# First batch worked by halves of the sequence, with an order written out by hand

## The chip, the core and the metric

The kernel runs on one core of a Trainium2 chip. The core has five engines with a queue each: TensorE (PE in the profile, with its weight loads listed apart as PEld), VectorE (DVE), ScalarE (ACT), GpSimd (POOL) and SyncE (SP), which here only issues transfers. The metric is the time of one execution in microseconds, lower is better; the median over several runs counts.

## What is computed

There are 4 batches, 8 heads, 768 positions and 64 columns per head. Keys are taken in 24 chunks of 32. Every query bounds its product with each chunk from above, keeps the six best causal chunks, and attends to these alone. The result, as rows of 512 columns, goes through a layer norm and a two-layer MLP with a residual.

```python
k_min, k_max = k_chunks.min(axis=3), k_chunks.max(axis=3)
ub = sum_d(max(q * k_min, q * k_max))            # [B,H,S,24], -1e9 where the chunk is not causal
top_chunks = argsort(ub)[..., -6:]
scores = where(selected & causal, q @ k.T / 8, -1e9)
x = (softmax(scores) @ v) as [B, S, 512]
xn = (x - mean(x)) / sqrt(var(x) + 1e-6) * g_ln
out = x + relu(xn @ w_ch1) @ w_ch2               # 512 -> 2048 -> 512
```

## The kernel before

Two heads make a pair, so there are 16 pairs `g`, four per batch. Positions are cut in six tiles of 128; the first three are half `r=0`, the last three half `r=1`.

Attention of one pair, by function:

- `load_qk` (L175) puts four transfers on SP, two for queries and two for keys, 192 KB each; `load_v` (L186) puts two on POOL.
- `turn` (L198) transposes query and key tiles on PE, four tiles and then two; a whole pair has 12 transposes at L202.
- `prep_q`, `prep_q2` (L207, L230) bring the queries to SBUF and split them for the bound: in float32 for batch 0, in two float16 parts later. `prep_k` (L243) reduces each chunk to its least and largest key (DVE, L251 and L252) and copies the keys (ACT, L253 and L254). `prep_b` (L256) builds the chunk matrix `BD`.
- `bounds` (L269) is PE: L280 in float32 for batch 0, L290 later, for position tiles 1 to 5. `select` (L296) finds the seventh largest bound (DVE, L307) and writes a mask `MN` (L308). `mask_t` (L313) transposes the mask and copies it into `QA` and `QB` (L318, L319), where it sits beside the queries so that the score matmul adds it.
- `scores` (L347) is PE at L359 and the exponential on ACT at L365, in six pieces per pair: two for half 0 and four for half 1. `diag` (L370) clears the upper triangle on POOL; `values` (L377) is PE at L385; `normalise` (L390) is DVE at L395 and L396 and writes `x_all`.

Then, per batch: `stats` (L405: L417 to L419), `rstd`, `x_t` (L431), `mlp1` (L446: PE at L454, ACT at L458) and `mlp2` (L462: PE at L467, DVE at L474, then the output on SP).

The order comes from numbers written beside each piece of work. `at(t, fn, ...)` records a piece at time `t`, the pieces are emitted in order of `t`, and a scheduler in the framework may still move instructions on each engine between them. One unit of `t` is about a pair. The pairs of batch 0 stand at `t` = -4 to 0 and their preparation before that; the MLP of batch 0 begins after the last of them, at `e = 4.0 * b`:

```python
e = 4.0 * b + (GAP if b > 0 else 0.0)
...
for m in range(KT2):
    at(e + 0.05 + 0.5 * d * m / KT2, mlp1, b, m // 8, 2 * m % KT2)
for n in range(24):
    at(e + 0.06 + 0.5 * d + 0.5 * d * n / 24, mlp2, b, n // 4, n % 4)
```

So batch `b`'s MLP lies among the attention of batch `b+1`, and the last batch's MLP stands alone. PSUM has eight banks: `ps_t` two for transposes, `ps_s` two for bounds and values, `ps_m` two pairs of banks that scores, `mlp1` and `mlp2` share.

The weights are loaded on POOL during batch 0: `w1_load` and `w2_load` first copy one element of a chunk reduction `kc` into the weight tile, so that the transfer starts no sooner than that reduction.

Of the kernel before, what the change touches and what calls it, by code (L numbers as in the profile page):

```python
# [19 lines left out]
def kernel(  # L20
# [21 lines left out]
    NR = 2  # L42
    TR = NT // NR
    HP = H // 2
# [16 lines left out]
    ldp = ctx.enter_context(tc.tile_pool(name="ldp", bufs=4))  # L61
    vap = ctx.enter_context(tc.tile_pool(name="vap", bufs=5))
# [3 lines left out]
    xp = ctx.enter_context(tc.tile_pool(name="xp", bufs=2))  # L66
    xcp = ctx.enter_context(tc.tile_pool(name="xcp", bufs=1))
    htp = ctx.enter_context(tc.tile_pool(name="htp", bufs=1))
# [3 lines left out]
    ps_t = ctx.enter_context(tc.tile_pool(name="ps_t", bufs=2, space=PSUM))  # L72
    ps_s = ctx.enter_context(tc.tile_pool(name="ps_s", bufs=2, space=PSUM))
# [4 lines left out]
    def at(t, fn, *args):  # L78
        pieces.append((t, len(pieces), fn, args))
# [7 lines left out]
    RT = const.tile([P, S], F16, name="RT", tag="RT")  # L87
    hsel = const.tile([P, 2], F32, name="hsel", tag="hsel")
    mhalf = const.tile([P, NT], F32, name="mhalf", tag="mhalf")
    NK = 5  # L90
# [17 lines left out]
    def consts_first():  # L108
        rr = RT[0:64, :]
# [9 lines left out]
        make_identity(nc, ident_f)  # L119
# [4 lines left out]
        )  # L124
        nc.gpsimd.memset(causf, 0.0)
# [4 lines left out]
        nc.vector.memset(hsel[0:64, 1:2], KS)  # L130
        nc.vector.memset(hsel[64:P, 0:1], KS)
        nc.vector.memset(hsel[0:64, 0:1], 0.0)
        nc.vector.memset(hsel[64:P, 1:2], 0.0)
        for i in range(NM):
            nc.vector.memset(MN[i], 0.0)
        for i in range(2):
            ring_init(i)
        nc.vector.tensor_copy(ident_h, ident_f)
        nc.vector.tensor_copy(ident_b, ident_f)

    def consts_late():
        nc.gpsimd.memset(mhalf, -0.5)
# [16 lines left out]
    def w2_load(j, g):  # L159
        nc.gpsimd.tensor_copy(w2b[0:1, 4 * j, 0:1], st[g]["kc"][0:1, 0, 0:1])  # L160
        nc.gpsimd.dma_start(w2b[:, 4 * j:4 * j + 4, :], w2_r[:, 4 * j:4 * j + 4, :])
# [5 lines left out]
    def xb(b):  # L167
        if b not in x_tiles:
            x_tiles[b] = (
                xp.tile([P, NT, H, D], F16, name="x_all", tag="x_all"),  # L170
                xp.tile([P, KT1, S], F16, name="xT", tag="xT"),
            )
        return x_tiles[b]

    def load_qk(g):  # L175
        b, hp = divmod(g, HP)
        for nm, src in (("qn", q), ("kn", k)):
            st[g][nm] = ldp.tile([P, NT, 2, D], F32, name=nm, tag=nm)
            if g == HP:
                nc.gpsimd.tensor_copy(st[g][nm][0:1, 0, 0, 0:1], st[HP - 1]["m8"][0:1, 0, 0, 0:1])  # L180
            for hh in range(2):
                nc.sync.dma_start(
                    st[g][nm][:, :, hh, :], src[b, 2 * hp + hh].rearrange("(t p) d -> p t d", p=P),
                )

    def load_v(g, t0, t1):  # L186
        b, hp = divmod(g, HP)
        if "va" not in st[g]:
            va = st[g]["va"] = vap.tile([P, 2, NT, 80], F16, name="va", tag="va")
            nc.gpsimd.memset(va[:, :, :, D:D + 1], 1.0)  # L190
        va = st[g]["va"]
        for hh in range(2):
            nc.gpsimd.dma_start(  # L193
                va[:, hh, t0:t1, 0:D],
                v[b, 2 * hp + hh, t0 * P:t1 * P, :].rearrange("(t p) d -> p t d", p=P),
            )

    def turn(g, nm, t0, t1):  # L198
        pst = ps_t.tile([P, 512], F32, name="tr", tag="tr")
        src = st[g][nm]  # L200
        for t in range(t0, t1):
            nc.tensor.transpose(pst[:, (t - t0) * P:(t - t0 + 1) * P], src[:, t, :, :], ident_f)  # L202
        return pst[:, 0:(t1 - t0) * P]
# [3 lines left out]
    def prep_q(g, t0, t1):  # L207
        whole = g < HP
        if t0 == 0:
            if whole:  # L210
                for nm in ("q32", "r32"):
                    st[g][nm] = prp.tile([P, S], F32, name=nm, tag=nm)
            else:
                for nm, tag in (("q", "q32"), ("r", "r32")):
                    t2 = prp.tile([P, 2, S], F16, name=nm + "2", tag=tag)
                    st[g][nm + "h"], st[g][nm + "l"] = t2[:, 0], t2[:, 1]
        pst = turn(g, "qn", t0, t1)
        c = slice(t0 * P, t1 * P)
        if whole:
            nc.scalar.copy(st[g]["q32"][:, c], pst)  # L220
            return
        qh, ql = st[g]["qh"], st[g]["ql"]
        u0 = max(t0, 1) * P
        u = slice(u0, t1 * P)
        nc.scalar.activation(qh[:, c], pst, ACTF.Copy, scale=QS)  # L225
        nc.vector.scalar_tensor_tensor(  # L226
            ql[:, u], pst[:, u0 - t0 * P:], QS, qh[:, u], op0=ALU.mult, op1=ALU.subtract,
        )
# [14 lines left out]
    def prep_k(g, t0, t1):  # L243
# [4 lines left out]
        if t0 == 0:  # L248
            st[g]["kc"] = smp.tile([P, 2, NCH], F32, name="kc", tag="kc")
# [311 lines left out]
```

## Time and profile before

| | |
|---|---|
| runs | 330.53, 334.00, 334.06 us; median 334.0 us |
| profiled execution | 332.52 us, span in the profile 330.8 us |
| PE busy / PEld busy | 301.0 us (91%) / 199.2 us (60%) |
| DVE, ACT, POOL busy | 203.9, 180.1, 74.0 us |
| first `mlp1` matmul (L454) | 60.5 us |
| first `mlp2` matmul (L467) | 98.6 us |
| transfers, q and k loads | 64 on SP, 192 KB each, 3.7 and 3.8 us to landing |
| transfers, w1 and w2 | 8 on POOL, 512 KB each, 7.8 and 8.2 us to landing |

A matmul's record spans its way through the array, and these ways overlap; 301 us busy is therefore not 301 us of work, and the time between starts in an unbroken row is what a matmul really occupies. The profile page also cuts the span into 40 slices of 8.27 us with the busy share of each engine in tenths. The chain of waits follows the end of the program back through what released each step.

### The profile page before, as it was taken

The page shows a single profiled execution, that of the slowest core. Times are in us where ns is not written, and L with a number is a line of the kernel's source. Part 1 is how long each engine was busy: PE and PEld are TensorE (multiplying, and loading weights), DVE is VectorE, ACT ScalarE, POOL GpSimd, SP SyncE. Part 2 cuts the span into 40 slices and gives each one's busy share as a digit, 9 for nine tenths or more (in the row PEclk, how much of TensorE's full clock was granted, in tenths as well). Part 3 has the DMA queues.
Part 4 walks back from the last instruction along what each step waited for, and adds up shares of the span by engine and source line. Part 5 has one row for each costly group of instructions (what it writes and reads, how often), then busy time and mean ns, then how long its engine had stood idle before and what let it go on. Part 6 is the DMA issues. An engine that isn't in the chain of part 4 may idle for free.

```text
span 330.8 us, 6794 instructions
## 1 busy us (share of the span) xinstructions
PE 301.0 (91%) x2708; PEld 199.2 (60%) x2708; DVE 203.9 (62%) x657; ACT 180.1 (54%) x261; POOL 74.0 (22%) x116
## 2 busy tenths in 40 slices
PE   3879887999999998999999999999999999899994
PEld 2668675666675664666766565666656455565441
DVE  7766755998857779896564759886634336700121
ACT  2436759677975475358685625377775332366000
POOL 9714835211131422230313131120101020100000
PEclk9999989999999999999999999999999999999999
DMA  9997999963435636424523050000000101000021
GB/s 163 190 187 139 194 195 214 190 146 68 95 26 127 96 93 104 92 45 95 74 51 24 34 87 34 34 33 2 2 0 2 63 34 63 35 0 2 32 95 63
DMA packets 81967, 26.65 MB, mean 81 GB/s; under 512 B 76304, under 2 KB 78352, under 8 KB 81936
## 3 DMA queue, kind: packets, MB, share of 16 engines
q1 hardware_dynamic: 53632, 18.88, 24.1%
q0 software_dynamic: 27776, 7.34, 22.2%
q8 instruction: 21, 0.34, 0.5%
q10 hardware_dynamic: 528, 0.00, 0.1%
q14 instruction: 10, 0.08, 0.1%
HBM read 27.27 MB, written 6.29 MB: 101 GB/s over the span
## 4 chain that ended last, share of the span: by engine, by line
PE 60%; ACT 19%; DVE 15%; issue 2%; DMA 1%; SPq 0%; POOL 0%; ACTq 0%
PE mm L454 20%; PE mm L467 18%; ACT pt L365 8%; PE mm L359 6%; ACT hT L458 5%; PE sm L385 4%; PE ub L280 4%; PE tr L202 3%; ACT KB L254 3%; ACT KA L253 2%; DVE ot L474 2%; PE ub L290 2%; DVE kc L251 2%; DVE kc L252 2%; PE trh L435 2%
## 5 line engine op out<-in xcount | busy, mean ns | idle before, releaser
L365 ACT ACTIVATE pt<-mm 128x1024 f16<-128x1024 f32 x96 | 86.8, 916 | 52.1 <-PE mm L359 51.5
L454 PE MATMUL mm<-xT,w1b 128*128 128x384 f16 x512 | 93.3, 326 | 4.7 <-ACT hT L458 3.2
L467 PE MATMUL mm<-w2b,hT 128*128 128x512 f16 x384 | 92.7, 379 | 2.5 <-DVE ot L474 1.7
L458 ACT ACTIVATE hT<-mm 128x768 f16<-128x768 f32 x64 | 51.8, 810 | 40.7 <-PE mm L454 40.2
L454 PEld LDWEIGHTS <-w1b 128*128 128x128 f16 x512 | 49.0, 98 | 32.3 <-issue 5.5
L467 PEld LDWEIGHTS <-hT 128*128 128x128 f16 x384 | 36.6, 98 | 37.0 <-issue 3.7
L372 POOL TENSOR_SCALAR_AFFINE_SELECT pt<-pt 128x768 f16<-128x768 f16 x32 | 28.2, 880 | 115.4 <-ACT pt L365 115.4
L474 DVE SCALAR_TENSOR_TENSOR ot<-mm,rstd,x_all 128x512 f32<-128x512 f32 x24 | 17.9, 745 | 44.6 <-PE mm L467 43.1
L359 PE MATMUL mm<-QA,KA 128*128 128x128 f16 (+2 forms) x224 | 35.9, 251 | 5.2 <-ACT pt L365 4.3
L359 PE MATMUL mm<-QB,KB 128*128 128x128 f16 (+2 forms) x224 | 35.4, 252 | 0.0
L385 PE MATMUL sm<-va,pt 128*128 128x65 f16 x672 | 33.0, 195 | 2.3 <-ACT pt L365 1.8
L385 PEld LDWEIGHTS <-pt 128*128 128x128 f16 x672 | 28.4, 99 | 9.4 <-ACT pt L365 3.5
L193 POOL DMA_DIRECT2D va<-in_v_dram x32 | 28.2, 883 | 1.1 <-issue 0.2
L395 DVE RECIPROCAL rden<-sm 128x6 f32<-128x6 f32 x32 | 6.2, 193 | 33.5 <-PE sm L385 33.4
L253 ACT CAST KA<-tr 64x512 f16<-64x512 f32 (+1 forms) x32 | 15.0, 468 | 17.3 <-DVE kc L252 17.2
L359 PEld LDWEIGHTS <-KA 128*128 128x128 f16 x224 | 19.0, 102 | 8.9 <-issue 2.3
L202 PE MATMUL tr<-ident_f,qn 128*128 128x128 f32 x96 | 18.7, 303 | 5.9 <-DMA qn<-in_q_dram 5.1
L359 PEld LDWEIGHTS <-KB 128*128 128x128 f16 x224 | 18.6, 101 | 6.7 <-issue 4.2
L202 PE MATMUL tr<-ident_f,kn 128*128 128x128 f32 x96 | 19.7, 306 | 1.6 <-DMA kn<-in_k_dram 0.7
L251 DVE TENSOR_REDUCE kc<-tr 128x16 f32<-128x512 f32 (+1 forms) x32 | 17.7, 552 | 3.1 <-PE tr L202 2.9
L396 DVE TENSOR_TENSOR x_all<-sm,rden 128x384 f16<-128x384 f32 x32 | 17.7, 555 | 0.8
L226 DVE SCALAR_TENSOR_TENSOR q<-tr,q 128x384 f16<-128x384 f32 (+1 forms) x24 | 11.7, 488 | 9.9 <-ACT q L225 9.6
(79 smaller groups left out, 339.8 us busy)
## 6 DMA issues: line engine op xcount, KB each, us to landing
qn<-in_q_dram SPq DMA_DIRECT2D x32, 192.0 KB, 3.7
kn<-in_k_dram SPq DMA_DIRECT2D x32, 192.0 KB, 3.8
out_dram<-ot SPq DMA_DIRECT2D x24, 256.0 KB, 2.0
va<-in_v_dram POOLq DMA_DIRECT2D x32, 96.0 KB, 5.2
w1b<-in_moe_w_ch_dram POOLq DMA_DIRECT2D x4, 512.0 KB, 7.8
w2b<-in_moe_w_ch_dram POOLq DMA_DIRECT2D x4, 512.0 KB, 8.2
gstr<-in_moe_g_ln_dram ACTq DMA_DIRECT2D x1, 2.0 KB, 3.4
```

What stands on the lines that cost most here:

```text
L193: nc.gpsimd.dma_start(va[:, hh, t0:t1, 0:D], v[b, 2 * hp + hh, t0 * P:t1 * P, :].rearrange("(t p) d -> p t d", p=P),)
L202: nc.tensor.transpose(pst[:, (t - t0) * P:(t - t0 + 1) * P], src[:, t, :, :], ident_f)
L251: nc.vector.tensor_reduce(kc[:, 0, n], view, axis=AX.X, op=ALU.min)
L253: nc.scalar.copy(KA[g % NK][0:64, c], pst[0:64, :])
L359: nc.tensor.matmul(sc[:, hh, o:o + w * P], ks[:, t * P:(t + 1) * P], qs[:, s * P:(s + w) * P], start=True, stop=True,)
L365: nc.scalar.activation(pt[:, n0:n1].rearrange("p n h x -> p h n x"), sc[:, :, 0:o].rearrange("p h (n x) -> p h n x", x=P), ACTF.Exp, scale ...
L372: nc.gpsimd.affine_select(out=dv, in_=dv, compare_op=ALU.is_ge, fill=0.0, base=0, pattern=[[0, 2 * TR], [1, P]], channel_multiplier=-1,)
L385: nc.tensor.matmul(pv[:, hh, s2, :], pt[:, where[t, s], hh, :], va[:, hh, t, 0:D + 1], start=(t == 0), stop=(t == s),)
L454: nc.tensor.matmul(hp_[:, i, 0:TR * P], w1b[:, kt, (m + i) * P:(m + i + 1) * P], xT[:, kt, c], start=(kt == 0), stop=(kt == KT1 - 1),)
L458: nc.scalar.activation(hts[b][:, m:m + 2, c], hp_[:, :, 0:TR * P], ACTF.Relu, scale=HS)
L467: nc.tensor.matmul(yp, hts[b][:, kt, s * P:(s + 1) * P], w2b[:, kt, :], start=(kt == 0), stop=(kt == KT2 - 1),)
L474: nc.vector.scalar_tensor_tensor(ot, yp, rs[b]["rstd"][:, s:s + 1], x_all[:, s].rearrange("p h d -> p (h d)"), op0=ALU.mult, op1=ALU.add,)
```

## The change

Batch 0 is no longer worked pair by pair. Its eight units are the four first halves of the sequence and then the four second halves, `u = 0..7`, `g = u % 4`, half `i = u // 4`. The list `begin` writes their order out by hand as steps `n` = -3 to 7: in step `n`, unit `n+3` is turned and reduced, unit `n+2` gets its bounds, unit `n+1` its selection and mask, unit `n` its scores, and unit `n-1` its values. At step 4 the first halves of all heads are done, and their layer norm, `x_t` and `mlp1` follow while the second halves are worked. For these pieces an added dependency ties every instruction on PE, DVE, ACT and POOL to the one before it, so that the scheduler can't move them against each other.

With it come:

- every load of queries and keys is half as long and there are twice as many; keys go first. The second-half keys of batch 0 are gated by a one-element copy on POOL (`load_qk`), and so are the weights;
- values of batch 0 are loaded in halves too; loads have places in a table `loads` by step;
- layer norm, transpose and MLP go by half for all batches: `x`, `xc`, `xT`, `hT` are tiles of a half. `x` is float32, before it was float16. In batch 0 the norm's statistics are taken per pair (`pair_stats`, three instructions of 128 columns a unit) and joined by `bn_aggr`;
- the ReLU of batch 0's queries goes from DVE to ACT, which reads the transposed queries in PSUM a second time;
- PSUM: one pool `ps_t` of four banks for transposes, bounds, values and `mlp2`; `ps_m` keeps its two pairs for scores and `mlp1`;
- eight matmuls on zeros (`warm`) before the first transposes; the exponential's table is asked for at the start (`tiny`); the identity is made before `RT`; `causf` is made later; four rings `QA`, `QB`, `KA`, `KB`, before five;
- `GAP` is 0.8, before 1.5, and MLP pieces of batch `b` lie between `e = 4b + 0.86` and `z = e + 4`: `mlp1` of half 0 in the first half of that stretch, `mlp1` of half 1 and `mlp2` of half 0 in the second, `mlp2` of half 1 in the two units after `z`. For batch 0, `mlp1` of half 0 comes before `e`.

```diff
-    ps_t = ctx.enter_context(tc.tile_pool(name="ps_t", bufs=2, space=PSUM))
-    ps_s = ctx.enter_context(tc.tile_pool(name="ps_s", bufs=2, space=PSUM))
+    ps_t = ctx.enter_context(tc.tile_pool(name="ps_t", bufs=4, space=PSUM))
     ps_m = ctx.enter_context(tc.tile_pool(name="ps_m", bufs=2, space=PSUM))
...
+    def load_qk(g, i):
+        b, hp = divmod(g, HP)
+        for nm, src in (("kn", k), ("qn", q)):
+            t = st[g][nm, i] = ldp.tile([P, TR, 2, D], F32, name=nm, tag=nm)
+            if g < HP and i == 1 and nm == "kn":
+                nc.gpsimd.tensor_copy(t[0:1, 0, 0, 0:1], st[min(g + 1, HP - 1)]["kc"][0:1, 0, 0:1])
+            for hh in range(2):
+                nc.sync.dma_start(...)
...
+    def q_copy(g, i):
+        pst = st[g]["qn", i]
+        if g < HP:
...
+            nc.scalar.copy(st[g]["q32"], pst)
+            nc.scalar.activation(st[g]["r32"][:, u:], pst[:, u:], ACTF.Relu)
...
+    def warm(n):
+        junk = ps_m.tile([P, 2, 512], F32, name="junk", tag="mm")
+        for i in range(n):
+            nc.tensor.matmul(junk[:, i % 2], MN[0][:, 0, :], ..., start=True, stop=True)
...
+    def pair_stats(g, r):
+        for i in range(TR):
+            nc.vector.bn_stats(h["st"][:, i, hp], xh(b, r)[:, i, 2 * hp:2 * hp + 2]...)
...
+    loads = {
+        -3: [(load_v, 0, 0), (load_v, 1, 0)],
+        -2: [(load_v, 2, 0)],
+        -1: [(load_v, 3, 0), (load_qk, 0, 1)],
+        0: [(w1_load, 0, 2), (w1_load, 1, 2), (load_qk, 1, 1)],
+        1: [(load_qk, 2, 1), (w1_load, 2, 3), (w1_load, 3, 3)],
+        2: [(load_v, 0, 1), (load_qk, 3, 1)],
...
+    for n in range(-3, U):
+        there = [0 <= n + d < U for d in range(4)]
+        g, i = zip(*[((n + d) % HP, (n + d) // HP) for d in range(4)])
+        if n > 0:
+            begin += last(n - 1)          # values, normalise, pair_stats
+        if there[0]:
+            begin += [(scores, g[0], i[0], 0), (scores, g[0], i[0], 1)]
+        if n == HP:
+            begin += [(stats, 0, 0, t) for t in range(TR)] + [(centre, 0, 0, t) for t in range(TR)]
+            begin += [(x_t, 0, 0, kt) for kt in range(KT1)]
+        if there[0] and i[0] == 0:
+            begin += [(diag, g[0], 0)]
+        if there[1]:
+            begin += [(select, g[1], i[1])]
+        if there[3]:
+            begin += [(turn, g[3], "kn", i[3]), (k_bound, g[3], i[3]), (k_diag, g[3], i[3])]
+            begin += [(turn, g[3], "qn", i[3]), (q_copy, g[3], i[3]), (k_copy, g[3], i[3])]
...
+        if there[1]:
+            begin += [(mask_t, g[1], i[1]), (mask_ring, g[1], i[1])]
+        if there[3]:
+            begin += [(q_ring, g[3], i[3])]
+        if there[2]:
+            a, z, _ = chosen(g[2], i[2])
+            begin += [(bounds, g[2], s, i[2]) for s in range(a, z)]
...
+        begin += loads[n]
...
+    for n, (fn, *args) in enumerate(begin):
+        pieces.append((-4 + 4.0 * n / len(begin), len(pieces), fn, args, True))
...
+        if b == 0:
+            spread(mlp1, b, 0, ready[0], e)
+            spread(mlp1, b, 1, e + 0.3, m)
+            spread(mlp2, b, 0, e, m)
+            spread(mlp2, b, 1, m, z)
+            continue
+        spread(mlp1, b, 0, e, m)
+        spread(mlp1, b, 1, m, z)
+        spread(mlp2, b, 0, m + 0.01, z)
+        spread(mlp2, b, 1, z + 0.01, z + 2.0)
...
+        for one in done[n:]:
+            if one.engine in (nc.tensor.engine, nc.vector.engine, nc.scalar.engine, nc.gpsimd.engine):
+                if one.engine in ahead:
+                    tc.add_manual_dep(one, ahead[one.engine], order, reason="order")
+                ahead[one.engine] = one.name
```

## The prediction

> **What bounds the kernel now.** I read the slices first, then each stage, then the chain of waits for what a matmul costs. The page's slices of 8.27 us; rows PE, DVE and granted clock:
>
> ```profile
> PE   3879887999999998999999999999999999899994
> DVE  7766755998857779896564759886634336700121
> PEclk9999989999999999999999999999999999999999
> ```
>
> PE is full from the eighth slice on and patchy before. The busy time by stage, cut where the first MLP matmul of batches 0, 1, 2, 3 starts (PE, PEld, DVE, ACT, POOL; clock; transfers), and below it three shorter stretches:
>
> ```profile
> 0.00:60.50 60.50, 45.18 (x444) 37.22 (x445) 40.41 (x143) 33.44 (x50) 32.81 (x66) 0.97 1.31 184
> 60.50:140.30 79.80, 76.45 (x757) 51.28 (x755) 65.08 (x210) 52.21 (x80) 17.85 (x24) 1.00 0.55 101
> 140.30:212.50 72.20, 69.75 (x673) 46.28 (x673) 50.61 (x165) 43.47 (x64) 13.79 (x18) 1.00 0.31 55
> 212.50:282.30 69.80, 67.05 (x608) 42.04 (x606) 38.24 (x122) 38.04 (x52) 8.25 (x9) 1.00 0.06 24
> 60.00:70.00 10.00, 9.75 (x79) 6.39 (x76) 9.72 (x29) 7.48 (x14) 1.84 (x4) 1.00 1.13 186
> 70.00:80.00 10.00, 9.55 (x96) 6.76 (x94) 8.41 (x31) 7.64 (x13) 1.40 (x2) 1.00 0.47 107
> 80.00:90.00 10.00, 9.45 (x91) 6.68 (x88) 8.15 (x29) 8.42 (x14) 1.66 (x2) 1.00 0.35 79
> ```
>
> Pieces of the chain of waits (start, length, what), unbroken rows of matmuls:
>
> ```profile
> 34.66 2.43 PE ub L280 x20
> 61.21 1.09 PE tr L202 x8
> 92.66 0.85 PE sm L385 x28
> 95.34 0.85 PE ub L290 x20
> 287.36 17.55 PE mm L454 x108
> 304.91 17.28 PE mm L467 x80
> ```
>
> Divided: mlp1 0.1625 us a matmul, mlp2 0.216, values 0.030, transposes 0.136, bounds 0.0425 (float16) and 0.122 (float32). By columns a 128-wide score or float16 transpose is 0.055. A pair's PE work is then 12 x 0.136 + 0.85 + 5 x 0.055 + 42 x 0.055 + 42 x 0.030 = 6.3 us (8.0 in batch 0, whose bounds take 2.5); x_t adds 1.35 a batch; MLP 512 x 0.1625 + 384 x 0.216 = 166.1. In all 166 + 33.5 + 3 x 26.7 = 280 us of the 330.8. The other 51 us: 33 us of work in the first 60.5 leaves 27.5 idle; the three mixed stages hold 205 us of work in 221.8, 17 idle (the second of them 68.2 in 72.2, 94.5%); the rest lies in the last stage, of which the last 4.1 us are the last output. So PE bounds the kernel after 60.5 us, and before it a chain does. Its waits in 0 to 60.5:
>
> ```profile
> ACT q L220 <- PE tr L202: 10.6, 3, 4.9
> DVE m L307 <- PE ub L280: 8.8, 4, 3.4
> ACT pt L365 <- PE mm L359: 8.1, 7, 3.6
> ACT KA L253 <- DVE kc L252: 5.4, 5, 2.0
> ```
>
> No engine leads: each stands waiting for another in turn, with DVE busy 40.41 of 60.5, 67%.
>
> **The change, part by part.** PE's work stays: the same transposes, scores and MLP, bounds in equal numbers (4 plus 6 pairs of instructions for 10), some extra causal matmuls (8 for 4, 0.1 each). What moves is where it lies.
>
> *The front goes by DVE.* One step of a first-half unit, from rows of before: L395 0.19, L396 0.555, three statistics of 128 columns; four maxima at 0.1 (ten take 1.0) and mask 0.25 (L308: 0.39 for 240); two reductions of 384 columns (0.55 each, between 0.42 for 256 and 0.69 for 512), 0.2 and 0.26 for the chunk matrix; two mask copies of 256 (0.28, L318: 0.495 for 640); two ring copies of 384 (0.35, L234/L235: 0.54 to 0.60 for 768). The statistics have no row of that size: at least 0.16 (the shortest like it, L418), at most 0.68 (L417, 512 columns); as reductions scale with columns I take 0.28. Sum 5.06; 5.45 with second-half selection. The centring now reads float32: 0.345 (float16 row L419) to 0.48 (L233, 640 float32 columns); I take 0.39.
> DVE starts its first reduction at 8.2 us: ident casts, RT at about 4.1, four rings at 0.84 + 0.22; before, it was 8.0. Steps -3, -2: 2.26 each; -1, 0: 3.47; 1, 2: 5.06; 3: 5.45; into step 4 up to the centred half 4.2: 31.3 us until the first mlp1 matmul. The rest of step 4 to 7, the end of batch 0 and what of pairs 4 and 5 stands among it in DVE's order: 26.3 more, 57.6 in all up to xT of the second half. PE needs 3.1 us of a first-half step (6 transposes, 8 float32 bounds, 10 scores, 12 values) and 5.1 of a second-half one, ACT 3.4 to 3.6 (exponentials 1.62, copies 1.42, ReLU about 0.45, which leaves DVE), and 5.7 in step 4. So DVE sets the pace. A pace without waits doesn't exist; the best comparison is 60 to 90 us of before, DVE 26.3 of 30, 87.6%, in the same company of transposes, selections and matmuls. Then first mlp1 at 8.2 + 31.3/0.876 = 44 us (60.5 before), and end of batch 0's attention E = 8.2 + 57.6/0.876 = 74.
>
> By then PE has done 33.5 + 10.4 (mlp1 of half 0, 64 matmuls) + 3.3 (six half-turns and one bounds of batch 1) = 47 us; idle in the front 27 instead of 27.5, but with 13.7 us more work behind it at 74 than at 60.5. That alone is nothing gained; what counts is what comes after.
>
> *The middle.* Left after E, before the last attention is done: 280 - 47 - 52 = 181 us on PE. DVE's share of it is light: its total 204 + 4, less 65 done and 11 in the tail (15 outputs at 0.745), is 132; ACT's is less. Ratio DVE/PE is 0.73, as in the second mixed stage (50.6/68.2); I take that stage's 94.5%: 191.5 us. The first mixed stage, where DVE had to catch up (65.08), goes away. mlp2 leaves the pairs of banks that scores use; scores then never find one of the two taken. Waits of scores and mlp1 for a free pair cost PE 0.7 + 2.3 us in the mixed stages, so this is worth 3 us at most and I count none of it: mlp2's bank is now taken from the four of transposes, bounds and values.
>
> *The tail.* After the last values PE still has mlp2 of batch 2's second half and all of batch 3: 3 x 16 x 0.216 + 41.5 = 52 us, without DVE or ACT in the way; 1.5 for the stop at the last half's layer norm (before: 0.96 and 0.84 us), then 4.1 to the end. Before it was 42 us of work in 44.4.
>
> *Queues.* SP issues 128 loads for 64, at 0.5 us (0.81 to 1.84: two in 1.03) 32 us more, under 280 us in which SP mostly waits; the price shows where the data is late, see the first rival. In POOL's queue eight diagonals, eight weight loads, the gates and the value loads of batch 0 are in one row. Eight matmuls on zeros lie in the wait for the first load (PE's first 5 us are empty), 0.
>
> Sum: 74 + 191.5 + 52 + 1.5 + 4.1 = 323.1 us span against 330.8. The profiled run took 332.5, 1.7 more than its span, and its median neighbour 334.0. Forecast 324.8 us.
>
> *A rule against it.* PE has 3.1 us of work in a first-half step of 5.8. Before, it fell to half clock in such a stretch (columns as above, granted clock third from the end):
>
> ```profile
> 44.00:46.00 2.00, 1.09 (x10) 1.03 (x10) 1.35 (x5) 1.34 (x2) 1.07 (x3) 1.00 1.24 205
> 48.00:50.00 2.00, 2.00 (x24) 1.81 (x22) 1.51 (x13) 1.02 (x1) 1.11 (x3) 0.50 1.24 206
> ```
>
> At half clock a first-half step is 6.2 us on PE, 0.4 over 5.06/0.876 = 5.8; four such steps cost 1.6 us, which I leave to the range. The Trainium skill (TensorE: Matmul & The Clock Gate, Part 1) lets the clock fall only after an idle window of about 3.4 us. By that rule the sum has no such term; here the longest gap ahead of the fall was 1.24 us, so the row speaks for the range.
>
> **Rivals.**
>
> 1. *Slower: the keys come late.* Second-half keys of pairs 1 to 3 wait for a gate in POOL's queue, behind the step's diagonal, behind ACT's exponentials, and behind weight loads. From a step's start: exponentials done at 3.0, diagonal 0.88, two weight loads with gates 1.5, gate 0.17, SP 0.5, landing 3.8 (median row of kn) to 7.8 (w1b, in the same crowd): 9.9 to 13.9. They are turned 1.1 us into the step after next, 12.7 at my pace. At the slowest landing of w2b, 10.9, they are 4.3 us late in each of steps 2, 3 and 4: E = 87, time 338. It decides from 7.7 us of lateness in all, where E passes 81.7 and the time 332.5. For it: transfers move 184 GB/s over all of 0 to 60.5, more than in any later stage. Against: the halves are 96 KB where 192 took 3.8.
> 2. *No change: three full engines.* From 44 to 74 us the orders hold PE 28, DVE 26 and ACT 28 us of 30, none of which can wait for another. With E = 77 and the third mixed stage's 92% (64.3 in 69.8) for the middle, 196.7: 333 us.
> 3. *Much faster.* DVE at the 97% of 60 to 70 us gives E = 67.6; banks of their own give the middle 98%, 184.7: 311.6 us. Against: nothing in before kept both for long.
>
> That the order isn't what the change says is no rival: the emitted order has all eight mlp1 pieces of half 0 ahead of the second half's x_t.
>
> **How the numbers follow.** Forecast (318 to 330.6) 0.47, much faster 0.20, no change 0.15, slower 0.18. One per cent is about what a measurement of this kernel tells from no change (its runs spread from 330.53 to 334.06); so faster 0.67, same 0.15, slower 0.18. The range leaves a tenth out on each side: 312 to 340, with statistics at 0.68 (24 x 0.4 = 9.6 us on DVE) inside.
>
> **What would show it.** First L490 (mlp1) at 44 us; last xT of batch 0 at 74; last attention value 57.6 us before the span's end; DVE above 80% from 10 to 70 us; no clock of 0.5 after 15 us. Wrong: PE waiting for a kn transfer in steps 2 to 4, or the middle over 197 us with waits of PE for a bank.

## The result, and the profile after

The changed kernel takes 345.32 us (median of 4 runs, 343.13 to 345.52), the kernel before 332.65 us in runs on the same chip. The ratio is 1.037, with a 95% interval from 1.030 to 1.044: slower, where faster was forecast. In this and all later ratios and intervals, runs more than 1.5% above the fastest of the same kernel are left out; the medians are over all runs. The profiled execution took 343.13 us, with a span of 341.4 us against 330.8 before.

The slices of the changed kernel, 8.54 us each, rows PE, DVE and granted clock:

```profile
PE   6693869869599999988779999999999999999995
DVE  7972586566884758899987657996664167010011
PEclk9655589999999999999999999999999999999999
```

Slice four (25.6 to 34.1 us) is the first thing to see: PE falls to 3, and the clock row stands at 5 around it. DVE, which was to be above 80% from 10 to 70 us, never holds that. The stages, cut at the prediction's own milestones (first `mlp1`; last xT of batch 0's second half; last values; end), and two stretches of the front. Columns as before: PE, PEld, DVE, ACT, POOL; then granted clock, share of the transfer engines, GB/s:

```profile
0.00:50.60 50.60, 33.51 (x236) 28.16 (x237) 35.12 (x131) 22.16 (x42) 24.60 (x53) 0.68 0.96 158
50.60:87.70 37.10, 31.20 (x343) 22.65 (x342) 23.91 (x93) 25.59 (x38) 18.64 (x30) 0.98 1.07 123
87.70:284.30 196.60, 183.61 (x1863) 123.70 (x1863) 142.28 (x449) 123.66 (x176) 36.42 (x47) 1.00 0.29 58
284.30:341.40 57.10, 52.89 (x287) 26.92 (x282) 12.23 (x25) 12.98 (x16) 0.85 (x1) 1.00 0.13 47
20.00:30.00 10.00, 7.82 (x64) 7.05 (x63) 7.17 (x31) 5.00 (x9) 3.73 (x10) 0.50 1.01 187
30.00:40.00 10.00, 4.60 (x26) 4.40 (x27) 2.65 (x8) 1.70 (x4) 1.94 (x4) 0.50 0.85 155
```

From 30 to 40 us no engine is busy for half of the time (PE 4.60 of 10 us, DVE 2.65, ACT 1.70), while transfers go on at 155 GB/s. That is the look of a wait for data. The waits of the first 50.6 us name it (engine, line, waited for; us in all, times, longest):

```profile
ACT q L222 <- PE tr L211: 9.5, 4, 6.4
DVE kc L259 <- PE tr L211: 6.9, 2, 6.1
PE tr L211 <- DMA kn<-in_k_dram: 6.7, 2, 6.0
```

Read from the bottom: PE's longest wait, 6.0 us, is for a key transfer (`kn` is a loaded key tile); DVE and ACT wait 6.1 and 6.4 us for the transposes behind it. The same moment in PE's timeline, and then SP's (start, length; idle time before in brackets):

```profile
34.60 0.87 PE L211 MATMUL tr<-ident_f,kn 128*128 128x128 f32 x3 [5.97 <-DMA kn<-in_k_dram]
```

```profile
13.58 0.47 SPq L191 DMA_DIRECT2D kn<-in_k_dram  x1
14.15 10.54 SPq L191 DMA_DIRECT2D qn<-in_q_dram  x6
24.79 6.20 SPq L191 DMA_DIRECT2D kn<-in_k_dram  x4
```

The late tile is pair 1's second-half key. Its gate on POOL had been passed at 20.90 us. But on SP it stood behind query loads, the last of them one of batch 1, which waits for PE to transpose an earlier tile out of its buffer; SP came to the key at 24.79 us. Four weight loads (issued at 19.30, 20.37, 24.60 and 25.62 us) shared the transfer engines with it, and the key landed at about 34.5: 9.7 us after its issue, where the median of these loads is 2.6. So it was late twice, in the queue and on the way.

Milestones against the forecast: first `mlp1` 50.6 us for 44, end of batch 0's attention 87.7 for 74, middle 196.6 for 191.5, tail 57.1 for 57.6.

**Where the difference lies.** Stages that hold different work can't be compared, so I cut all kernels at points where the attention done is the same, the first normalising (`rden`) of batches 1, 2 and 3, the last one, and the end, and count the MLP matmuls done in each piece, at the prediction's 0.1625 and 0.216 us. Each cell is the time, and in brackets the MLP work, in us. The lower four are experiments told below.

| kernel | to batch 1 | to batch 2 | to batch 3 | to the last | to the end |
|---|---|---|---|---|---|
| before | 85.1 (14.3) | 63.1 (31.1) | 72.9 (41.6) | 60.4 (37.0) | 49.3 (42.1) |
| changed | 100.5 (14.7) | 64.9 (31.5) | 63.6 (31.7) | 55.5 (36.7) | 57.0 (51.5) |
| early keys | 92.0 (14.7) | 64.9 (31.4) | 63.6 (31.8) | 55.5 (36.7) | 57.0 (51.5) |
| old front, new banks | 89.0 (14.3) | 63.9 (32.1) | 73.3 (41.5) | 57.3 (36.1) | 47.5 (42.1) |
| old batch 0, new rest | 87.4 (14.3) | 63.4 (30.5) | 62.2 (32.4) | 56.1 (37.4) | 57.2 (51.5) |
| old batch 0, old banks | 85.1 (14.3) | 63.0 (29.8) | 65.5 (33.0) | 63.0 (37.5) | 58.8 (51.5) |

Time less MLP work, changed against before: 15.1 us lost before batch 1, 1.3 and 0.5 in the next two pieces, then 4.6 gained up to the last normalising and 1.7 in the tail. That is +10.6, the difference of the spans. So the loss is in the front, and the work that was brought forward there bought nothing: at 100.5 us the changed kernel has done no more MLP than the one before at 85.1.

### The profile page after: what moved, and what is told of

It reads as the page before. It is cut to its first block, busy times and chain, and to the rows that moved or that the text cites. A ratio compares the mean times of both kernels' runs of the same rounds, so it can differ in the third digit from the quotient of the medians.

```text
span 341.4 us, 6996 instructions
## 1 busy us (share of the span) xinstructions
PE 301.2 (88%) x2720; PEld 201.4 (59%) x2720; DVE 213.5 (63%) x698; ACT 184.4 (54%) x270; POOL 80.5 (24%) x130
## 4 chain that ended last, share of the span: by engine, by line
PE 58%; DVE 27%; ACT 8%; DMA 3%; issue 2%; POOL 1%; SPq 0%; ACTq 0%; POOLq 0%
PE yp L502 20%; PE mm L490 16%; PE mm L386 6%; PE tr L211 5%; PE sm L412 4%; ACT pt L392 3%; DVE bst L454 3%; PE ub L306 3%; DMA kn<-in_k_dram 3%; PE ub L296 2%; DVE kc L260 2%; DVE xc L460 2%; DVE x L422 2%; DVE kc L259 2%; PE trh L475 1%
## 5 line engine op out<-in xcount | busy, mean ns | idle before, releaser
L490 PE MATMUL mm<-xT,w1b 128*128 128x384 f16 x512 | 96.7, 327 | 3.0 <-ACT hT L494 1.5
L502 PE MATMUL yp<-w2b,hT 128*128 128x512 f16 x384 | 95.9, 379 | 0.0
L490 PEld LDWEIGHTS <-w1b 128*128 128x128 f16 x512 | 49.3, 98 | 34.5 <-issue 5.2
L508 DVE SCALAR_TENSOR_TENSOR ot<-yp,rstd,x 128x512 f32<-128x512 f32 x24 | 17.9, 747 | 52.5 <-PE yp L502 50.7
L202 POOL DMA_DIRECT2D va<-in_v_dram x40 | 33.1, 834 | 1.3 <-issue 1.1
L412 PE MATMUL sm<-va,pt 128*128 128x65 f16 x672 | 27.5, 196 | 1.3 <-ACT pt L392 1.0
L259 DVE TENSOR_REDUCE kc<-tr 128x12 f32<-128x384 f32 x32 | 17.5, 548 | 13.1 <-PE tr L211 13.1
L264 ACT CAST KA<-tr 64x384 f16<-64x384 f32 x32 | 14.9, 466 | 8.1 <-DVE kc L260 7.8
L211 PEld LDWEIGHTS tr<-ident_f,kn 128*128 128x128 f32 x96 | 12.7, 154 | 11.2 <-issue 6.6
L232 ACT ACTIVATE q<-tr 128x384 f16<-128x384 f32 x24 | 11.8, 491 | 11.9 <-PE tr L211 11.7
L422 DVE TENSOR_TENSOR x<-sm,rden 128x384 f32<-128x384 f32 x32 | 17.7, 554 | 0.7
```

The source lines that it names most:

```text
L202: nc.gpsimd.dma_start(st[g]["va"][:, hh, a:z, 0:D], v[b, 2 * hp + hh, a * P:z * P].rearrange("(t p) d -> p t d", p=P),)
L211: nc.tensor.transpose(pst[:, t * P:(t + 1) * P], src[:, t], ident_f)
L259: nc.vector.tensor_reduce(kc[:, 0, n], view, axis=AX.X, op=ALU.min)
L412: nc.tensor.matmul(pv[:, hh, s2, :], pt[:, where[t, s], hh, :], va[:, hh, t, 0:D + 1], start=(t == 0), stop=(t == s),)
L422: nc.vector.tensor_tensor(xh(b, r)[:, :, 2 * hp:2 * hp + 2, :].rearrange("p s h d -> p h s d"), pv[:, :, :, 0:D], rden.to_broadcast([P, 2, ...
L490: nc.tensor.matmul(hp_[:, i, 0:TR * P], w1b[:, kt, (m + i) * P:(m + i + 1) * P], h["xT"][:, kt], start=(kt == 0), stop=(kt == KT1 - 1),)
```

## The experiments

Each was run beside the kernel before, whose median in these groups of runs lies between 330.8 and 332.6 us; so a difference of less than 2 us between experiments of different groups isn't resolved by the times alone. "Early keys" and "the zeros" name two of the edits, on which later ones stand.

### The late key and the clock

*The order on SP.* The changed kernel's order pins four engines, not SP:

```diff
-if one.engine in (nc.tensor.engine, nc.vector.engine, nc.scalar.engine, nc.gpsimd.engine):
+if one.engine in (nc.tensor.engine, nc.vector.engine, nc.scalar.engine, nc.gpsimd.engine, nc.sync.engine):
```

> The loads of q and k of batch 0 and the first of batch 1 are issued on SP in the order in which they are written; every other queue keeps its order. Late-key theory: the key half of pair 1 no longer stands behind a query load of batch 1 that waits for PE, so PE's wait of 6.0 us for kn goes; first mlp1 at 44.6 us for 50.6, end of batch 0's attention 82 for 87.7, time 339.5 for 345.3. Clock theory (PE at half clock from 10 to 41 us sets the pace, the late key is hidden behind it): the wait for kn goes, but PE is still at half clock for over 25 us and the time falls by 2 us at most, to 343.

Measured: 339.18 us (ratio to before 1.022, 1.015 to 1.029), 6 us less than the changed kernel. The wait for kn fell to 2.0 us, first `mlp1` came at 45.7, the end of batch 0's attention at 83.1. The clock still averaged 0.52, 0.67 and 0.62 in the three stretches of ten from 10 to 40 us. The late-key theory had 44.6, 82 and 339.5 us, and is met within 1.1 us; but it had the wait gone, and 2.0 us of it stayed, although SP issued the key at 21.24 us, right behind its gate (21.04):

```profile
29.05 0.88 PE L211 MATMUL tr<-ident_f,kn 128*128 128x128 f32 x3 [2.03 <-DMA kn<-in_k_dram]
```

*The clock.* Zeros, from a tile of their own, through PE in the first eight steps (shortened):

```diff
+if n < 5: begin += [(warm, 4)]     # after mask_t, and again after bounds
```

> 64 matmuls on zeros (two groups of four in each of the first eight steps) keep TensorE busy. Clock theory: the granted clock stays at full from 10 to 41 us, PE's waits of DVE and ACT shrink, first mlp1 at 45 us for 50.6, time 340. Late-key theory: the wait of 6 us for kn stays where it is (28.6 to 34.6 us, since the load is issued after SP's queue is free), only the stretch after it gets faster: first mlp1 at 48.5, time 343. The zeros may themselves cost PE 0.2 us each where PE is not idle, 2 to 4 us at most.

Measured: 339.10 us (1.023, 1.016 to 1.030). The windows (columns as above) show that the clock was cured from the second stretch on:

```profile
10.00:20.00 10.00, 9.32 (x61) 6.39 (x61) 8.19 (x30) 5.97 (x14) 2.63 (x6) 0.83 1.15 161
20.00:30.00 10.00, 8.07 (x88) 6.14 (x87) 7.88 (x33) 5.71 (x11) 4.60 (x12) 1.00 0.92 175
30.00:40.00 10.00, 8.84 (x90) 6.69 (x89) 7.76 (x28) 4.92 (x10) 5.14 (x9) 1.00 1.11 186
```

But the wait for kn had gone too, to 1.1 us, which the late-key theory had denied. SP's queue shows why:

```profile
14.21 6.14 SPq L193 DMA_DIRECT2D qn<-in_q_dram  x4
20.40 5.33 SPq L193 DMA_DIRECT2D kn<-in_k_dram  x4
```

A faster PE turned the earlier query sooner, SP came through its query loads at 20.40 us and not 24.79, and the key was nearly in time. So this run doesn't tell the two theories apart; it took both together, and one without the zeros.

> Both edits together. If the late key and the half clock are the two causes of the front's loss: first mlp1 at 44 us, as forecast, end of batch 0's attention 76 to 78, time 333 to 335. If second-half steps are bound by the chain between PE, ACT and DVE (scores in four pieces that wait for one another), then first mlp1 at 44 but end of attention at 81 or later, and 338.

Measured: 347.29 us, with runs spread from 342.0 to 349.8 (1.039, 1.027 to 1.051). Its profiled execution, 347.69 us, has PE waiting 4.3 us for the query half that stands in SP's pinned order behind the gated key of the same pair: SP issued it at 22.57 and 23.11 us, among the weight loads, and PE could turn it at 33.64. Pinning SP removed one way to be late, not the lateness itself. What made the spread so large isn't settled.

*Early keys.* SP's order, and no gate:

```diff
-if g < HP and i == 1 and nm == "kn":
-    nc.gpsimd.tensor_copy(t[0:1, 0, 0, 0:1], st[min(g + 1, HP - 1)]["kc"][0:1, 0, 0:1])
```

> SP's loads in the order written, and the gates ahead of the second-half keys of batch 0 taken away: these loads go as soon as a buffer is free, ahead of the weights of the MLP, in a stretch (15 to 20 us) in which the transfers stood still. No zeros added. Late-key theory: PE waits for kn and qn under 1 us after 12 us, first mlp1 at 44 to 45, time 337 to 339. If the order on SP alone did it: as with SP's order alone, 339. If the first loads suffer from the company: first step 1 to 2 us later, 341.

Measured: 334.86 us (1.008, 1.004 to 1.013), 10.5 us less than the changed kernel, and better than any of the three expectations. PE waits for no kn; the key half that was turned at 34.60 us is turned at 26.80:

```profile
26.80 0.49 PE L209 MATMUL tr<-ident_f,kn 128*128 128x128 f32 x3
```

Its stages:

```profile
0.00:41.80 41.80, 31.89 (x236) 26.89 (x237) 35.18 (x131) 22.30 (x42) 24.08 (x49) 0.78 1.15 185
41.80:79.10 37.30, 31.39 (x342) 22.67 (x341) 23.89 (x93) 25.48 (x38) 18.60 (x30) 0.97 1.09 129
79.10:275.80 196.70, 183.69 (x1863) 123.75 (x1864) 142.41 (x450) 123.65 (x176) 36.33 (x47) 1.00 0.30 58
```

First `mlp1` comes at 41.8 us, 8.8 earlier than in the changed kernel and 2.2 earlier than forecast, and all that follows keeps its length to 0.2 us (37.3 for 37.1, 196.7 for 196.6). Keys in time are worth 8.8 us in that place and nothing elsewhere. And this with the clock still at half for much of the time (0.50 from 10 to 20 us, 0.82 and 0.83 in the next two stretches). It was at half for less of it than in the changed kernel (0.78 in the mean up to first `mlp1`, there 0.68), and what of the 8.8 us belongs to that isn't parted.

> The same with 64 matmuls on zeros in the first eight steps. If late loads were what made SP's order and the zeros together slow (347), this has no such wait: first mlp1 at 43 to 44, end of batch 0's attention 81 to 82, time 335.5 to 338. If something else made that pair slow, it is slow here too: 342 or more.

Measured: 338.97 us (1.019, 1.013 to 1.025), 4 us more than without zeros. Clock 1.00 from 10 to 40 us, no wait for kn, first `mlp1` at 43.9. With the keys in time, full clock bought by zeros loses more than it gives: at the 0.216 us of an `mlp2` matmul, which has 512 columns too, 64 zeros hold PE for an estimated 13.8 us. So the half clock doesn't explain why first `mlp1` came later than forecast, since early keys beat the forecast with it; what full clock would be worth if it cost nothing on PE stays open.

### DVE in the middle

```diff
-x_tiles[b, r] = xp.tile([P, TR, H, D], F32, name="x", tag="x")
+x_tiles[b, r] = xp.tile([P, TR, H, D], F16, name="x", tag="x")
```

> x of the attention is kept in float16, as before the change. DVE saves 24 x 0.16 us on the centring, 3.9 us in all, of it 0.6 to 1 us per stage. If DVE bounds the mixed stages of batches 1 and 2: 1.5 to 3 us off, 342.5 to 344. If PE's wait at each layer norm is what counts: 12 waits get shorter by up to 0.5 us each, also 2 to 4 us. If DVE has slack: within 0.5 us of 345.3.

Measured: 343.82 us (1.037, 1.031 to 1.043). DVE's busy time fell from 213.5 to 209.5 us, as expected. In its profile a kn load was late by 10.0 us (issued at 23.24 us, turned at 35.70), so only what follows can be compared. From 88.3 to 285.6 us it takes 197.3 us, the changed kernel 196.6; but that stretch begins with a piece in part at half clock (0.77 up to batch 1's first normalising, in the changed kernel 1.00). Between points of equal work, batch 1's first normalising and the last one, first the changed kernel, then, in two pieces, this one:

```profile
100.52:284.40 183.88, 173.94 (x1765) 116.78 (x1764) 131.20 (x416) 116.45 (x164) 34.69 (x45) 1.00 0.29 57
```

```profile
88.30:103.25 14.95, 12.50 (x103) 9.02 (x102) 11.03 (x35) 7.65 (x14) 1.72 (x2) 0.77 0.34 71
103.25:285.67 182.42, 174.08 (x1766) 116.82 (x1764) 128.57 (x417) 116.44 (x164) 34.52 (x45) 1.00 0.29 57
```

There 2.6 us less on DVE go with 1.5 us less time. That is the lower end of what was expected if DVE bounds the mixed stages, and the time lies in that range too, so DVE may have a small part in the middle; one profile of each kernel is thin ground for 1.5 us.

> On top of the zeros (339.1 us): batches 1 to 3 get their MLP spread as before the change, both halves of the first layer in the first half of a batch's stretch and the second layer in the second half, none carried over into the next batch, and attention runs 0.7 units later against the MLP. Theory of DVE-bound mixed stages (PE 57.7 us of work beside 57 to 59 of DVE in each of batches 1 and 2): more matmuls beside DVE's work, 3 to 5 us off, 334 to 336. If the middle's idle time is the stop at each half's layer norm (xc, 4.5 us on PE) or the wait of scores for exponentials: no gain, 338 to 341.

```diff
-GAP = 0.8
+GAP = 1.5
-spread(mlp1, b, 0, e, m); spread(mlp1, b, 1, m, z)
-spread(mlp2, b, 0, m + 0.01, z); spread(mlp2, b, 1, z + 0.01, z + 2.0)
+spread(mlp1, b, 0, e, e + 1.0); spread(mlp1, b, 1, e + 1.0, m)
+spread(mlp2, b, 0, m + 0.01, m + 1.0); spread(mlp2, b, 1, m + 1.0, z)
```

Measured: 343.64 us (1.033, 1.026 to 1.039), 4.5 us more than with the zeros alone: both expectations missed. The end of batch 0's attention came 5 us earlier, at 77.9, with batch 1's preparation placed later, and all that follows took 9 us longer. The theory that more matmuls beside DVE's work would help isn't borne out. The edit changes GAP and layout at once, so it doesn't say which of the two lost.

### What makes the second-half steps long

With the keys in time, steps 4 to 7 still take 37.3 us where 30 were forecast. Two theories: waits for exponentials in a chain, or too much work (batch 1's preparation, the early MLP).

> On top of the zeros (339.1 us): the first layer of batch 0's first half no longer runs beside the second halves' attention, but after it (10.4 us of PE work moved). If PE's work sets those four steps (44.8 to 83 us): batch 0's attention ends 8 to 10 us earlier, at 73 to 75, and the time stays within 1 us of 339. If the chain of scores, exponentials, values and normalising sets them and the MLP only fills its gaps: the end moves by 2 us at most, to 81, and the time grows by 8 us to 347.

```diff
-spread(mlp1, b, 0, ready[0], e)
+spread(mlp1, b, 0, ready[1], e)
```

Measured: 338.30 us (1.016, 1.010 to 1.023), 0.8 less than with the zeros alone. Its profiled execution took 344.20 us, far from that, so only the times are used; the same edit on the early keys has one that can be used:

> On top of the early keys: the first layer of batch 0's first half after the second halves' attention, not beside it. If PE's work in steps 4 to 7 sets them (31.4 busy of 37.3 us): the end at 70 to 72, time 334 to 336. If the chain sets them and the MLP fills gaps: end at 76 to 79, and the 10.4 us of work come after it, time 340 to 344. The same edit on top of the zeros gave no change (338.3 for 339.1), which speaks for a middle that has room.

Measured: 333.34 us (1.005, 1.001 to 1.009), no more than with the early MLP (1.5 us less, which isn't resolved), where the chain theory had 340 to 344. First the steps, from the first copy of xT on DVE, in early keys, then the same without the early MLP, and there from their end to the first normalising of batch 1:

```profile
41.18:79.14 37.96, 32.02 (x347) 23.13 (x346) 24.35 (x94) 26.09 (x39) 19.22 (x31) 0.96 1.10 130
```

```profile
42.80:76.60 33.80, 27.00 (x308) 20.92 (x306) 24.28 (x94) 21.91 (x34) 19.37 (x31) 0.91 1.07 130
76.60:92.50 15.90, 15.90 (x145) 11.06 (x143) 10.64 (x34) 12.03 (x19) 1.92 (x3) 1.00 0.56 88
```

Of the 64 matmuls 28 are still done by 76.6 us, since the scheduler lets pieces slip in, so 36 of them, 5.9 us, were moved. The steps got 4.2 us shorter, and idle time on PE in them went from 5.9 (38.0 less 32.0) to 6.8 us. So more than half of the early MLP lay on the path and less than half in gaps. What was moved out was done directly after, with PE full (15.90 of 15.90), and batch 1's first normalising comes at 92.5 us, against 92.0. Beginning the MLP early is worth nothing that these runs resolve.

> On top of the early keys (334.9 us; first mlp1 at 41.8, end of batch 0's attention at 79.1): in the second-half steps the values of a step are issued after the first two score pieces of the next one, not before them, so PE has work while ACT and POOL finish the exponentials. Chain theory (steps 4 to 7 wait for exponentials, 4.1 us of PE waits for pt in them): the end moves to 75 to 77, time 331.5 to 333.5. Batch-1 theory (the steps are long because batch 1's transposes, bounds and selection lie among them): end within 1 us of 79, time 334 to 336. Should the values come too late for the normalising, which DVE then does later: slower, 336 to 338.

```diff
-if n > 0:
+if n > 0 and n <= HP:
     begin += last(n - 1)
 if there[0]:
     begin += [(scores, g[0], i[0], 0), (scores, g[0], i[0], 1)]
+if n > HP:
+    begin += last(n - 1)
```

Measured: 336.25 us (1.013, 1.005 to 1.021), 1.4 more than early keys. PE's waits of scores for exponentials fell from 3.5 to 1.0 us up to 90 us, and waits of the mask transposes for DVE grew from 1.5 to 7.3 us: the end of batch 0's attention stayed at 79.2. A stall was moved, not removed.

> On top of the early keys: GAP 1.4 for 0.8, so the preparation of batch 1 and all that follows stands 0.6 units later; the MLP keeps its shape. Batch-1 theory: the end of batch 0's attention at 74 to 75, as forecast before (the run with GAP 1.5 had it at 77.9 with first mlp1 at 44.6); what left those steps comes after the end, so the time gains 1 us at most or loses: 333.5 to 337. Chain theory: end at 78 to 79, and the time 335 to 338.

Measured (GAP 1.4 for 0.8): 336.37 us (1.013, 1.006 to 1.020). The end of batch 0's attention came at 75.1 us, 4.0 earlier and close to the 74 of the forecast; the first normalising of batch 1 came at 93.7, 1.7 later. As the batch-1 theory said for the place, and for the time: nothing gained. But the clock averaged 0.82 from that end to that normalising, where early keys has 1.00, so a part of the 1.7 us may be the clock's.

> Early keys, values one place later, GAP 1.2 together: if both work, the end at 73 to 75 and the time 329 to 332, which would be below the kernel before; if either is a wash, 333 to 336.

Measured (GAP 1.2): 340.61 us (1.025, 1.017 to 1.034), outside both expectations. Two edits of 1.4 and 1.5 us add up to 5.8; why isn't settled. Its clock stood at 0.50 from 30 to 40 us, where early keys has 0.83.

Over early keys and the four variants without zeros that stand on it, the end of batch 0's attention moves between 75 and 81 us, and the time doesn't follow it. The point that counts is the first normalising of batch 1, which none of the four brought below 92.0. There early keys still stands 6.9 us behind the kernel before (85.1), with the same MLP work done; no run here shows what takes these 6.9 us.

### The later batches on the old front

In the kernel before, three edits. Banks: `ps_t` with four banks in place of `ps_t` and `ps_s`, second-layer sums in them. Layout: hidden tiles by halves (with them a third buffer for `x_all`), MLP spread as in the changed kernel. Place: GAP 0.8.

```diff
-    ps_t = ctx.enter_context(tc.tile_pool(name="ps_t", bufs=2, space=PSUM))
-    ps_s = ctx.enter_context(tc.tile_pool(name="ps_s", bufs=2, space=PSUM))
+    ps_t = ctx.enter_context(tc.tile_pool(name="ps_t", bufs=4, space=PSUM))
...
-            yps[b] = ps_m.tile([P, 2, 512], F32, name="mm", tag="mm")
+            yps[b, s] = ps_t.tile([P, DM], F32, name="yp", tag="one")
...
+        spread(mlp1, b, 0, e, m); spread(mlp1, b, 1, m, z)
+        spread(mlp2, b, 0, m + 0.01, z); spread(mlp2, b, 1, z + 0.01, z + 2.0)
```

> The kernel before with its own front, and of the change only what concerns the later batches: the second layer's sums in banks of the common pool, and the MLP by halves with the second half's second layer carried into the next batch. From the point of equal work (first normalising of batch 1) the kernel before needs 245.7 us, the changed one 240.9. If that 4.8 us belongs to the layout and the front alone loses: 326 to 329. If the two can't be parted (the gain was only work pushed out of the front): 331 to 334.

> The kernel before with the banks alone: transposes, bounds, values and second-layer sums share four banks, the pairs are left to scores and the first layer; the order is as before. If the pairs were what cost PE its 3 us in the mixed stages: 328 to 330. If it is the layout that gains: 330.5 to 332.5, no change. If the shared banks cost transposes their turn: 333 to 335.

> As the old front with the new middle, with the 0.8 of the change for GAP instead of 1.5, so that batch 1 follows closer on batch 0. If the tightness is part of the gain: 1 to 2 us less than with 1.5, 325 to 327. If batch 1's preparation then lies in the front's way, as it did among the second halves (4 us there): 328 to 332.

Measured: 334.59 us (1.010, 1.007 to 1.014) for banks and layout, 332.85 (1.003, 0.999 to 1.007) for the banks alone, 336.83 (1.016, 1.012 to 1.021) with GAP 0.8. None gains. The banks alone lose 4 us before batch 1 (89.0 for 85.1) and gain 4 in the last batch and the tail. In the first, the same cut shows the place: batch 0's MLP, which stands at full density in the kernel before, was thinned as well, and at batch 1's first normalising (89.6 us) only 7.8 us of MLP were done, where the kernel before had 14.3 at 85.1: 11 us lost; later pieces gained it back in part. So the layout was kept from batch 1 on, and batch 0 left as it was:

> The kernel before with its front and its MLP of batch 0; the changed kernel's banks, and its layout of the MLP by halves for batches 1 to 3 alone. From the first normalising of batch 2 on (equal work) the changed kernel needs 5.8 us less than the one before; the banks cost the old front 4 us in the run with them alone. If both hold, 329 to 331; if the 4 us were chance, 326 to 328; if the layout brings nothing without the new front, 332 to 335.

> The same with the banks of the kernel before (second-layer sums in the pairs). If the layout is what gains after batch 2's first normalising: 325 to 328, below both kernels. If the banks are what gains there (the run with them alone gained 4.9 us in the last batch and the tail): 330 to 333.

Measured: 329.75 us with the new banks, ratio 0.993 (0.990 to 0.997), the only kernel here that beats the one before; 335.40 us with the old banks, 1.014 (1.009 to 1.019). The last batch, from its first normalising to the last, first with new banks, then with old:

```profile
213.08:269.20 56.12, 55.70 (x533) 35.84 (x532) 30.00 (x90) 34.88 (x47) 5.17 (x6) 1.00 0.07 25
```

```profile
213.50:276.50 63.00, 59.24 (x535) 36.32 (x534) 29.69 (x91) 35.50 (x46) 5.20 (x7) 1.00 0.07 26
```

The same work, 0.4 us idle on PE against 3.8. With old banks PE waits for pairs of banks, scores and `mlp1` in turn behind exponentials, ReLU and outputs:

```profile
PE mm L454 <- ACT pt L365: 1.9, 4, 0.7
PE mm L359 <- ACT hT L458: 0.6, 1, 0.6
PE mm L454 <- DVE ot L474: 0.4, 1, 0.4
```

With new banks one wait of 0.2 us is left. Idle time explains 3.3 of the 6.9 us. The rest is hidden in PE's busy time, whose records overlap: counted from start to start, 86 matmuls of the second layer take 23.6 us with old banks, 87 take 19.6 with new ones, and the 156 of the values 7.0 for 4.8; why the values take longer isn't settled (the two profiled executions stand 1.6 us below and 1.6 us above their medians). The change's gain in the later batches thus needs the banks; the layout adds to it only with them, since with old banks it costs 4 us. And the gain doesn't need the first batch's new order.

## Why the prediction was wrong, point by point

The span was forecast at 323.1 us and measured at 341.4: 13.7 more in the front, 5.1 more in the middle, 0.5 less in the tail. The first of the prediction's two signs of being wrong came true, PE waiting for a kn transfer in step 2.

- **The front, E = 74: measured 87.7.** This is the step that failed, in two places. Up to the first `mlp1`, 44 was forecast and 50.6 measured; with the keys in time it is 41.8. The prediction let DVE's sum of 31.3 us set the pace at 87.6%. Without the late key DVE is busy for 29.3 of the 33.6 us from 8.2 to 41.8, 87%: the pace was right and the sum 2 us too large (its prices are lengths of records, and these overlap a little). What was missing from the forecast was the wait for keys.
- **Rival 1, the late keys,** gave E = 87 and 338 us. E was right to 0.7 us, by luck: one wait of 6.0 us in step 2 with what it drew after it and steps 4 to 7 that were too long, not 4.3 us of waiting in each of three steps. Of the causes it named, gate and weight loads were real: with SP's order put right alone, 2.0 us of the wait stayed and first `mlp1` came at 45.7; with the gate gone too, ahead of the weights, at 41.8. What it missed was SP's queue, worth the other 4.9 of the 8.8 us. The prediction costed the gate, the weight loads and the landing, but put SP at 0.5 us, "under 280 us in which SP mostly waits". SP waited in order: a query load of batch 1, idle on a buffer, held up a key that was needed now. That SP's queue is not in the order written is a fact of the emitted program; the prediction spoke of PE's order alone.
- **Steps 4 to 7, 30 us from first `mlp1` to the end: measured 37.1.** The sum of PE's work, 28 us, was 31.2 us busy, and idle time 5.9 where it left 2. That E fell 7 us later than the orders' sums is the second failure of the front, and moving single pieces shifts it by 2.5 us (early MLP), 0 (values) and 4.0 us (batch 1) without a gain in time.
- **"What counts is what comes after": wrong.** The prediction let the front lose nothing and took 13.7 us of work done early as the gain. Equal work shows 15.1 us lost before batch 1's first normalising. Taking the early MLP away made the kernel no slower.
- **The middle, 191.5: measured 196.6.** The mechanism was right, PE's work with a share of idle time, and the size wrong: 181 us of work were to fill 94.5% of it, as in before's best mixed stage, and fill 92%. PE's busy time says the same, 93.4% (183.6 us) where that stage had 96.6% (69.75 of 72.20). DVE may have a part in it, some 1.5 us by the run with float16. That new banks were counted as nothing was too cautious: on the old front with the layout by halves they made 5.7 us (335.40 to 329.75).
- **The tail, 57.6: measured 57.1.** Right.
- **The small prices.** Pair statistics 0.28 us taken, 0.281 measured (24). Centring from float32 0.39 taken, 0.506 measured in the mean (0.456 in the median, a few are far longer), above the upper bound of 0.48; it cost DVE 2.8 us more than the sum had.
- **The half clock** was left to the range with 1.6 us. It lasted 30.7 us, longer than the four steps of 6.2 us that it was priced for. Its own price isn't shown: zeros that cured it took more time on PE than they gave, and early keys met the 44 us of the forecast with the clock at 0.78. The prediction took before's front for one at full clock, with 33 us of work and 27.5 idle; PE is busy there for 45.2 of 60.5 us, at half clock up to 26 us (last section).
- **Full engines (rival 2)** had E = 77, middle 196.7, 333 us: with the late key gone the kernel measures 79.1, 196.7 and 334.9. So without late keys "no change" would have been nearly the case (1.008). The reason given isn't what the rows show: from 41.8 to 79.1 us PE was busy for 31.4 of 37.3 us, ACT for 25.5, DVE for 23.9, so not three engines were full, and the agreement is partly luck.

## What to carry to other kernels

Compare two orders at points where the same work is done, not at the first instruction of a new stage: a stage that starts 10 us sooner has gained nothing if batch 1's first result comes 15 us later. When transfers are cut in pieces and their order is left to a scheduler, read the queue that issues them, and look in it for a load that waits for a buffer ahead of one that is needed now. Work moved into gaps of a front is only worth the gaps; here more than half of it lay on the path, and the room that it left later was not used.

## What the runs showed of the hardware that was not expected

The granted clock reads 1.00 where the trace has no record of it. The kernel before was thought to run its front at full clock; its durations say otherwise (a transpose of the keys from 8 to 26 us, then from 26 to 44):

```profile
L202 PE MATMUL tr<-ident_f,kn 128*128 128x128 f32 x12 | 3.7, 438 | 0.6 <-ACT q L220 0.5
```

```profile
L202 PE MATMUL tr<-ident_f,kn 128*128 128x128 f32 x8 | 1.5, 287 | 0.1
```

438 ns against 287, and bounds (L280) that start every 0.213 us between 13.4 and 17.5 us but every 0.112 us from 26.2 on: half clock up to about 26 us, then full. The first record of the clock in this trace lies at 26.1 us. So the 0.136 us of the prediction's transposes held only for the second part of before's front. The changed kernel, with its eight zeros ahead, began at full clock (transposes of 273 ns up to 11.1 us) and fell to half after an idle stretch on PE of 2.5 us (7.70 to 10.20): 421 ns from 11.5 to 41.9 us.

Nor did a busy PE bring the clock up. In the changed kernel it was busy for 7.97 of 8 us:

```profile
16.00:20.00 4.00, 4.00 (x27) 3.88 (x24) 2.97 (x13) 2.83 (x6) 1.69 (x4) 0.50 0.54 91
20.00:24.00 4.00, 3.98 (x33) 3.68 (x33) 3.37 (x15) 1.93 (x4) 1.59 (x4) 0.50 0.93 164
```

The clock stayed at 0.50 until 42 us. The Trainium skill (TensorE: Matmul & The Clock Gate, Part 1) has the clock rise after a busy window of about 3.4 us. These rows don't agree, unless "busy" is something other than what a profile counts as busy; float32 transposes and bounds 24 columns wide filled 4.3 of these 8 us. Matmuls of 512 columns on zeros, eight in each step, did hold it at 1.00 from 20 to 40 us.
